# A fused linear-attention and gated-unit kernel: fixed engine orders, a gate on four array tiles, row loads for two batches, and zero products during the fill

## The chip, the cores and the metric

One core of one Trainium2 chip. The metric is the device time of one execution in microseconds (us), the median of several executions. Engines: PE multiplies matrices (PEld is its weight load, which overlaps with products: 203.6 us of PE and 143.5 of PEld in the span of 248.5 before), DVE is VectorE, ACT is ScalarE, POOL is GpSimd, SP only issues transfers. A run counts as slow when it is more than 1.5% above the fastest run of the same kernel on that chip. Executions scatter by some 2% here (four of the kernel before took 247.9 to 254.9 us), so this label often marks ordinary scatter.

## The reference

```python
def phi(x):                                    # x: [8 batches, 8 heads, 576, 64]
    proj = np.einsum('bhsd,df->bhsf', x, w_phi)                    # w_phi: [64, 128]
    proj = proj - np.max(np.abs(proj), axis=-1, keepdims=True)
    return np.concatenate([np.exp(proj), np.exp(-proj)], axis=-1)
q_p, k_p = phi(q), phi(k)
kv = np.einsum('bhsf,bhsd->bhfd', k_p, v)                          # the "state"
num = np.einsum('bhsf,bhfd->bhsd', q_p, kv)                        # the "numerator"
x = num / (den + 1e-6)                                             # -> [8, 576, 512]
for k in range(5):                                                 # causal convolution in time
    gate_pre += conv_w[k] * xp[:, k:k + S, :]
return (sigmoid(gate_pre) * (x @ w_val)) @ w_out                   # float32 [8, 576, 512]
```

## The kernel before

Python code lists some 1200 operations with their dependencies; a planner gives each an engine and a place in that engine's order, then they are emitted with semaphores. An engine's instructions are emitted in the order of its list, and one that waits holds up those behind it. Per batch: k and q come transposed into SBUF, are projected and exponentiated (KTIL, QTIL on ACT), v is scaled (VT, on POOL), PE forms the state (KV) and numerator (NUM), transposes it (XT), then come gate (GATE), value (VAL) and output (OUT). "Fill" below is the time until the first numerator product.

Batch 0 gets k and q as plain rows, with PE transposes; a copy from PSUM then writes every ninth element (1.95 us for 384 of them on DVE). All other batches are cast to bfloat16 into DRAM by a POOL transfer and read back by a transposing transfer.

```python
def load(b):
    if b == 0:
        ...   # row load XF, cast XB, PE transpose T0, copy T0c with stride 9
    else:
        pl.op("cast", "POOL", ...)     # k, q -> bf16 in DRAM
        pl.op("tr", "SP", ...)         # DRAM -> KT / QT, transposed
...
def mlp(b):
    for jt in range(4):
        def mm(E, at, jt=jt):          # gate: 12 products of 288 columns, two column tiles
            return [E.matmul(m.PS[ROWS[hh], at + p, 0:HALF], m.DG[:, 2 * jt + hh, 3 * p + dl, :],
                XT[:, 2 * jt + hh, dl:dl + HALF], start=(dl == 0), stop=(dl == 2), ...)
                for p in range(2) for dl in range(3) for hh in range(2)]
```

## Time and profile before

| | before |
|---|---|
| median of 4 executions | 250.2 us (247.9 to 254.9) |
| span of the profiled execution | 248.5 us |
| first numerator product | 55.7 us |
| end of PE | 241.3 us |

How to read it: the kernel is a pipeline over batches. Time until the first numerator is the fill, in which PE waits; from then to its end PE is nearly always busy, so each microsecond it saves there counts; then come 7 us of last copies and stores. The prediction shows the lines that carry this.

### The profile page before, as it was taken

How to read it: one execution, taken by the hardware profiler on the slowest of the kernel's cores; microseconds unless marked ns; L12 is line 12 of the kernel's file. 1: busy time of each engine (PE TensorE's matmuls, PEld its weight loads, DVE VectorE, ACT ScalarE, POOL GpSimd, SP SyncE). 2: the span in 40 equal slices, each digit the busy share in tenths (PEclk: the TensorE clock that was granted, in tenths of full speed). 3: DMA queues.
4: the chain of work that ended last, by engine and by line, in shares of the span. 5: the costliest groups of instructions: out<-in, count | busy, mean ns of one | idle time of the engine just before them, and what ended most of it. 6: DMA issues, size and time to landing. Idle time of an engine off the chain costs nothing.

```text
span 248.5 us, 8457 instructions
## 1 busy us (share of the span) xinstructions
PE 203.6 (82%) x3708; PEld 143.5 (58%) x3708; DVE 183.3 (74%) x276; ACT 184.9 (74%) x250; POOL 120.5 (48%) x206
## 2 busy tenths in 40 slices
PE   2124357599879999999999999999949999999970
PEld 1022234377675668657765876686626866776720
DVE  2399599539469967996998799789954799368460
ACT  5356989989915789898989899989497988982300
POOL 7274049639820883668138818652386064700000
PEclk9999999999999999999999999999997999999996
DMA  6992492998699959795899599978996524003132
GB/s 242 275 176 92 79 278 40 156 182 131 102 193 218 264 106 287 183 223 135 196 184 256 112 286 143 165 200 212 206 211 119 171 73 146 0 10 122 45 108 103
DMA packets 54398, 39.94 MB, mean 161 GB/s; under 512 B 39381, under 2 KB 48725, under 8 KB 53850
## 3 DMA queue, kind: packets, MB, share of 16 engines
q1 hardware_dynamic: 52240, 30.03, 50.3%
q0 software_dynamic: 1952, 9.31, 21.8%
q8 instruction: 29, 0.48, 0.8%
q10 hardware_dynamic: 170, 0.08, 0.1%
q14 instruction: 7, 0.06, 0.1%
HBM read 30.48 MB, written 17.69 MB: 194 GB/s over the span
## 4 chain that ended last, share of the span: by engine, by line
PE 50%; ACT 15%; DVE 13%; DMA 11%; SPq 4%; POOL 2%; issue 2%; ACTq 0%; DVEq 0%
PE PS L909 10%; PE PS L936 8%; DMA VN<-in_v_dram 7%; PE PS L898 7%; PE PS L785 5%; ACT KTIL L617 5%; ACT QTIL L744 5%; PE PS L822 4%; DVE MQb L704 4%; DMA wtmp<-in_w_phi_dram 3%; DVE QT L587 3%; DVE MK L612 3%; PE PS L731 3%; PE PS L691 2%; ACT GS L904 2%; PE PS L607 2%
## 5 line engine op out<-in xcount | busy, mean ns | idle before, releaser
L653 POOL TENSOR_TENSOR VT<-VN,EK 128x512 bf16<-128x512 f32 x64 | 65.7, 1045 | 18.6 <-DMA VN<-in_v_dram 15.1
L617 ACT ACTIVATE KTIL<-PS 128x1024 bf16<-128x1024 f32 x64 | 62.9, 1039 | 11.3 <-PE PS L607 8.3
L744 ACT ACTIVATE QTIL<-PS 128x1024 bf16<-128x1024 f32 x64 | 62.5, 1028 | 4.5 <-PE PS L737 3.7
L704 DVE TENSOR_REDUCE MQb<-PS 128x8 bf16<-128x1024 f32 (+1 forms) x40 | 44.2, 1110 | 11.9 <-PE PS L691 8.7
L612 DVE TENSOR_REDUCE MK<-PS 128x8 f32<-128x1024 f32 x32 | 38.7, 1216 | 8.6 <-ACT KTIL L617 4.5
L914 DVE SCALAR_TENSOR_TENSOR GV<-GS,PS 128x576 bf16<-128x576 bf16 x32 | 24.0, 751 | 17.7 <-PE PS L909 12.8
L909 PE MATMUL PS<-XT,WV 64*128 64x288 bf16 x512 | 35.7, 284 | 1.1 <-ACT OS L585 0.4
L641 POOL TENSOR_SCALAR MK<-MK 128x16 f32<-128x16 f32 (+1 forms) x24 | 6.0, 251 | 59.8 <-DVE MK L612 48.6
L936 PE MATMUL PS<-WO,GV 128*128 128x512 bf16 x128 | 32.1, 380 | 0.2 <-DVE XT L845 0.2
L898 PE MATMUL PS<-XT,DG 128*64 128x288 bf16 x384 | 28.6, 297 | 0.8 <-ACT GS L904 0.5
L909 PEld LDWEIGHTS PS<-XT,WV 64*128 64x128 bf16 x512 | 24.3, 94 | 7.8 <-issue 0.9
L904 ACT ACTIVATE GS<-PS 128x576 bf16<-128x576 f32 x32 | 20.8, 664 | 8.4 <-PE PS L898 6.0
L898 PEld LDWEIGHTS PS<-XT,DG 128*64 128x64 bf16 x384 | 20.5, 112 | 8.6 <-DVE XT L879 1.3
L691 PE MATMUL PS<-W,QT 64*128 64x128 bf16 x256 | 14.6, 239 | 10.7 <-ACT QT L585 4.0
L836 DVE TENSOR_TENSOR XN<-PS,RC 128x512 bf16<-128x512 f32 x32 | 21.9, 689 | 0.7
L607 PE MATMUL PS<-W,KT 64*128 64x128 bf16 x256 | 13.9, 240 | 10.0 <-DVE KT L587 7.0
L785 PE MATMUL PS<-VT,KTIL 128*128 128x65 bf16 x512 | 20.7, 196 | 0.2
L785 PEld LDWEIGHTS PS<-VT,KTIL 128*128 128x128 bf16 x512 | 18.9, 99 | 1.5 <-issue 0.5
L822 PEld LDWEIGHTS PS<-KVSB,QTIL 128*128 128x128 bf16 x512 | 17.3, 97 | 3.8 <-ACT QTIL L744 0.7
L822 PE MATMUL PS<-KVSB,QTIL 128*128 128x65 bf16 x512 | 19.3, 193 | 0.0
L585 ACT ACTIVATE OS<-PS 128x512 f32<-128x512 f32 x23 | 13.9, 609 | 6.2 <-PE PS L936 6.2
L691 PEld LDWEIGHTS PS<-W,QT 64*128 64x128 bf16 x256 | 8.8, 103 | 15.5 <-issue 8.3
(77 smaller groups left out, 298.2 us busy)
## 6 DMA issues: line engine op xcount, KB each, us to landing
VN<-in_v_dram SPq DMA_DIRECT2D x16, 512.0 KB, 7.4
out_dram<-OS SPq DMA_DIRECT2D x32, 256.0 KB, 3.1
R<-in_q_dram POOLq DMA_DIRECT2D x14, 288.0 KB, 6.3
R<-in_k_dram POOLq DMA_DIRECT2D x14, 288.0 KB, 5.6
QTIL<-in_k_dram SPq DMA_DIRECT2D x2, 576.0 KB, 5.7
QTIL<-in_q_dram SPq DMA_DIRECT2D x2, 576.0 KB, 8.4
VNt<-in_v_dram SPq DMA_DIRECT2D x32, 32.0 KB, 3.4
out_dram<-OS SPq DMA_DIRECT2D x16, 64.0 KB, 2.7
```

Source lines behind the costliest of these rows:

```text
L612: pl.op("Kmax", "DVE", dve(1024), lambda E, at, u=u: [E.tensor_reduce(MK[:, 0, 8 * u:8 * u + 8].rearrange("p (t x) -> p t x", t=2), m.PS[: ...
L617: pl.op("Kexp", "ACT", act(1024), lambda E, at, u=u, g=g: [E.activation(KTIL[:, g, u, :, :, :], m.PS[:, at:at + 2, :].rearrange("p t (x f) ...
L653: pl.op("VT", "POOL", pool(512), lambda E, at, u=u, hh=hh, a=a, g=g, EK=EK: [E.tensor_tensor(m.VT[s][:, g, u, :, :, 0:D], m.VN[s][:, 4 * h ...
L691: res.append(E.matmul(m.PS[:, at + par, P * x:P * x + P], QT[ROWS[par], 4 * hh + x, P * j:P * j + P], m.W2[ROWS[par], :], start=True, stop ...
L704: pl.op("Qmax", "DVE", dve(256 * nx), lambda E, at, u=u, nx=nx: [E.tensor_reduce(MQb[:, :].rearrange("p (t s) -> p t s", t=2)[:, :, 4 * u: ...
L744: pl.op("Qexp", "ACT", act(1024), lambda E, at, u=u, g=g: [E.activation(m.QTIL[s][:, g, u, :, :, :], m.PS[:, at:at + 2, :].rearrange("p t ...
L785: res.append(E.matmul(m.PS[:, at + sg, x * E1:(x + 1) * E1], m.KTIL[s][:, sg, 2 * g + a, par, x, :], m.VT[s][:, sg, 2 * g + a, par, x, :], ...
L822: return [E.matmul(m.PS[:, at + g, x * E1:(x + 1) * E1], m.QTIL[s][:, sg, 2 * j + g, par, x, :], m.KVSB[s][:, g, sg, x, :], start=(sg == 0 ...
L898: return [E.matmul(m.PS[ROWS[hh], at + p, 0:HALF], m.DG[:, 2 * jt + hh, 3 * p + dl, :], XT[:, 2 * jt + hh, dl:dl + HALF], start=(dl == 0), ...
L904: pl.op("TANH", "ACT", act(576), lambda E, at, GS=GS: [E.activation(GS[:, :, :], m.PS[:, at:at + 2, 0:HALF], AF.Tanh, scale=0.5)], pr, w=[ ...
L909: return [E.matmul(m.PS[:, at + p, 0:HALF], m.WV[ROWS[p], h, P * jt:P * jt + P], XT[ROWS[p], h, PAD:PAD + HALF], start=(h == 0), stop=(h = ...
L936: return [E.matmul(m.PS[:, at, :], m.GV[jt][:, s, p, P * j:P * j + P], m.WO[:, jt, :], start=(jt == 0), stop=(jt == 3)) for jt in range(4)]
```

## The change

Four intents: (1) the orders of all engines come from a search and are written into the kernel, with earliest times for transfers; (2) the gate uses 64x64 tiles, meant to run four at once, so that each of the five taps is multiplied once instead of six padded ones (20 products for 12 a tile, in two phases that add into the same PSUM banks); (3) batches 0 and 1 come by row loads and PE transposes whose copies are contiguous; (4) PE multiplies zeros while it waits in the fill, meant to keep its pace up: in the fill of the kernel before, eight products of L737 take 0.43 us, at 58.7 us 0.24. Some copies also move from DVE to ACT. Cut to its core:

```diff
-    pl.weigh(CFG)
-    pl.schedule(CFG["limit"], CFG["bonus"])
+    pl.schedule(ORDER, LATE)              # five lists of operation numbers, earliest times of transfers
...
-        if b == 0:
+        if b < 2:                         # row loads, PE transposes, contiguous copies
...
+            for n in range(4):            # two tiles y, each in phase 1 (taps 0, 2, 4) and phase 2 (1, 3)
+                y, ks = n % 2, ((0, 2, 4), (1, 3))[n // 2]
+                def mm(E, at, jt=2 * a + y, ks=ks):
+                    for k in ks:
+                        for hh in range(2):
+                            for par in range(2):
+                                h, dl = 2 * jt + hh, k // 2 + (k & 1) * (1 - par)
+                                res.append(E.matmul(m.PS[ROWS[hh], at + (par ^ (k & 1)), 0:HALF],
+                                    m.DG[ROWS[par], h, k, :], XT[ROWS[par], h, dl:dl + HALF],
+                                    start=(k == 0), stop=(k == 3), ...))
+                ... mode="T", sync=gate[-2:-1] if n > 1 else []   # phase 2 waits for its phase 1
...
+    def warm(E, k):                       # 137 of these, all before 40 us of the plan
+        E.matmul(m.PS[:, 7, 0:2 * P], m.Z[0:k, 0:P], m.Z[0:k, :], start=True, stop=True, ...)
```

## The prediction

> **What bounds the kernel now.** I read the page first (busy shares and the 40 slices), then sums over stretches of the span, then the chain that ended last in order of time, then the groups of instructions by form. From the page:
>
> ```profile
> PE 203.6 (82%) x3708; PEld 143.5 (58%) x3708; DVE 183.3 (74%) x276; ACT 184.9 (74%) x250; POOL 120.5 (48%) x206
> ...
> PE   2124357599879999999999999999949999999970
> ...
> ACT  5356989989915789898989899989497988982300
> ...
> DMA  6992492998699959795899599978996524003132
> ```
>
> No engine is near 100% over the span, but the PE row splits it: a fill of some nine slices of 6.2 us in which PE is mostly idle, then nines with one dip (slice 30), then the end. The sums over stretches (columns: stretch, its length, then busy us and instructions of PE, PEld, DVE, ACT, POOL; granted clock; DMA share; GB/s) give the sizes:
>
> ```profile
> 43.00:56.00 13.00, 9.96 (x181) 7.30 (x177) 6.24 (x8) 11.74 (x15) 7.14 (x13) 1.00 1.01 167
> 56.00:81.00 25.00, 22.30 (x443) 16.59 (x436) 19.21 (x32) 16.28 (x25) 13.56 (x24) 1.00 0.95 163
> 131.00:156.00 25.00, 24.47 (x480) 17.02 (x477) 21.80 (x35) 23.34 (x34) 16.59 (x29) 1.00 0.92 195
> 181.00:200.00 19.00, 15.62 (x292) 11.32 (x293) 11.98 (x15) 16.52 (x23) 9.41 (x17) 0.91 0.69 150
> ```
>
> In the steady stage PE is busy 24.5 of 25 us, so the PE stream is the bound there. Asked for 81 to 181 us as one stretch, PE is busy 98.55 of 100 us with 1908 products; the eight batches have about 455 each (3708 less the setup, divided by 8), so a batch takes 23.8 us. DVE and ACT are at 86% there and DMA at 93%: three followers are close behind. In the fill the chain of waits is another one (start, us, what):
>
> ```profile
> 2.05 8.48 DMA wtmp<-in_w_phi_dram
> ...
> 10.90 3.44 DVE KT L587 x2
> ...
> 16.27 3.43 DVE QT L587 x2
> ...
> 20.48 1.88 ACT QT L585
> ...
> 23.48 3.54 ACT KT L585 x2
> ...
> 43.23 0.43 PE PS L737 x8
> ...
> 54.91 0.71 DVE KVSB L799
> ...
> 58.71 0.24 PE PS L737 x8
> ```
>
> The reader sees: the projection weight lands only at 10.5 us; then transposed copies of k and q go one after another; the first numerator product (L856) starts at 55.66 us. The same eight products of L737 take 0.43 us in the fill and 0.24 us at 58.7. The groups carry the unit costs:
>
> ```profile
> L587 DVE COPY QT<-PS 128x384 bf16<-128x384 bf16 x4 | 7.0, 1949 | 0.0
> L845 DVE COPY XT<-PS 128x1024 bf16<-128x1024 bf16 x16 | 10.8, 682 | 0.4
> L898 PE MATMUL PS<-XT,DG 128*64 128x288 bf16 x384 | 28.6, 297 | 0.8 <-ACT GS L904 0.5 <-DVE XT L845 0.3
> L476 ACT ACTIVATE EB<-I 128x2304 bf16<-128x2304 bf16 x1 | 2.1, 2122 | 0.0
> ```
>
> [...] sixteen products of L822 take 0.59 us after another mode and 0.49 us after their own, so 0.1 us. No run yet shows four tiles at once. [...] The copies of L587 write every ninth element and take 1949 ns for 384 elements, against 682 ns for 1024 contiguous ones at L845. That is 7.6 times as much an element, [...] I use the measurement.
>
> **The change part by part.**
>
> *Row loads and PE transposes for batches 0 and 1.* Removed: 12 strided copies at 1.9 us, 13.5 us of it on DVE (7) and 9 on ACT (5); four of 28 casts to DRAM and four of 28 DMA transposes (batch 1). Added: 24 copies of contiguous halves, 16 of 512 elements and 8 of 128. Batch 0's twelve casts stay but go mostly to POOL (7 of 12, where 3 were). From L845, 512 elements cost DVE about 0.35 us, or 0.6 for the q halves, whose order changes; ACT about 0.5. In all some 9 us for both engines instead of 22.6. The broadcast table of 2304 columns (2.1 us on ACT) becomes a broadcast view. The weight is loaded first, on a queue ahead of q. So the first exponential, 15.5 us before, should come at about 7.5: load landed 4.5 (as the first k load does now, at 4.4), cast, transpose, copy and product with 0.5 to 1 us each.
>
> From there ACT sets the fill. In the new order it has, ahead of the first numerator, the 16 exponentials of k of batches 0 and 1 and 2 tails each (about 17 us at 0.93 dense and 0.5), those of q of batch 0 (8.4), some of q of batch 1 (3), about 11 copies (5) and small ones (1.5): 35 us. 7.5 + 35 + 1.5 for waits gives 44 us for the first numerator, in place of 55.7. That is **11.7 us**, nearly all of it on the path. ACT has no room to do better, so the zero products (137) and the warm clock by themselves are worth little, 1 us: PE waits for ACT in the fill, warm or not.
>
> *The gate.* Per tile of 128 channels, 12 products of 288 columns on two column tiles (0.86 us with the switch, 0.75 without) become 20 on four tiles. Five taps by 288 columns at the rate of the value product (16 products of 288 in 0.99 us, two at a time, so 123 ns per pair) make 0.62 us, 31 ns a product; the trace issues one each 30 ns in L785, so issue just holds. 32 x 0.12 = **3.8 us**, all on the PE stream, the bound of the steady stage. I expect PE busy in this group to fall from 28.6 to about 23 to 25 us.
>
> *Order.* Mode changes on PE are 174 before and 168 after, and after the first numerator 153 and 141: 12 x 0.11 = **1.3 us**. The work behind the first numerator, each product at its dense rate and each change at 0.11, comes to 172.8 us before and 167.4 after. Before, it took 185.7 us (55.7 to 241.4): 7.5% over. About 5 us of that are one stall, 181 to 192, where the v load lands at 178 and PE waits, then runs cold. New orders start loads at chosen points and should lose most of that stall. At 3 to 4% over, 167.4 becomes about 173 us.
>
> *Moved.* Seven of 16 state copies, five of eight small ones and four output copies go from DVE to ACT: some 7 us less on DVE, 5 more on ACT. Neither is the steady bound.
>
> *Sum.* 44 + 173 + 7.1 (end of PE to end of span, as before) = 224 us of span. Measured times lie about 2 us over the span (250.5 for 248.5), but the order tables were searched and may overlap more than I count. I say **225 us**.
>
> **The rivals.**
> *DMA becomes the bound.* It is 93% busy in the steady stage, some 22.2 us of DMA a batch; PE work falls to about 22.5 to 23. If loads queue, v lands late and the stall at 181 returns, perhaps twice, at 5 us each: 230 to 235. For it: two waits of 9 us on v in the chain. Against: batch 1's DRAM round trip is gone, and loads are timed.
> *The fill starves.* Each engine's order is fixed, batches 0 and 1 are interleaved, and three queues load at once. If batch 1's row loads are late, transposes of batch 1 hold up products of batch 0 on PE. The first numerator then comes at 48 to 52 us: 229 to 233. Against: 4.7 MB of inputs at some 250 GB/s are in by 20 us, and PE needs batch 1 only after all of batch 0's k.
> *The tiles don't overlap.* If only two of the four tiles run at once, 20 products take 1.2 us a tile in place of 0.75, and 32 tiles lose 15 us instead of gaining 4: 240 or so. For it: no trace of this kernel has four tiles. Against: two column tiles do overlap now.
> *ACT becomes the bound.* Its dense work is about 180 us (128 exponentials at 0.93, 32 tails at 0.5, 32 gates at 0.55, 27 output copies at 0.5, some 14 of small ones); with 7.5 before and 20 behind it is 208 at least, so it can't set the end unless it waits a lot. This is also the floor of any gain.
>
> **Range and chances.** The fill is fairly sure (8 to 14 us), the gate (0 to 4) and the stall (0 to 6) less so, and the order could give some us beyond. All good makes 215; fill and stall bad makes 236. The three runs of before spread from 247.9 to 254.9, so a miss of 2 us is noise. A time within 2% or above needs the gate to fail badly and the fill to starve. Faster 0.97, same 0.02, slower 0.01.
>
> **What would show it.** Right: first numerator at 42 to 46 us; copies into KT and QT at 0.3 to 0.65 us in place of 1.9; the gate at some 0.6 us per 20 products; no stretch after 60 us with PE below 90%; steady batch at 22.5 to 23.3 us; L737's successors as short in the fill as later. Wrong: DMA at 1.0 over many slices with PE waiting on VT or KT; PE waiting in the fill for batch 1's loads; gate products over 45 ns each; a low granted clock in the middle.

44 us to the first numerator, 173 to the end of PE and 7.1 behind it make 224 us of span, and the time said was 225. 0.11 us for a mode change, an estimate, agrees with the gate's 0.86 less 0.75 us; the products of L822 gave 0.1.

## More of the kernel before

One more stretch of the fill before, from the sums over stretches (columns: stretch, length, busy us and instructions of PE, PEld, DVE, ACT, POOL, granted clock, DMA share, GB/s), matters later:

```profile
6.00:43.00 37.00, 15.40 (x208) 10.13 (x210) 29.27 (x30) 27.05 (x33) 17.01 (x29) 1.00 0.65 158
```

While it fills, the DMA share of the kernel before is 0.65.

## The result, and the profile after

The changed kernel takes 236.9 us in the median (236.6 to 239.0, four fast runs) against 250.2 us. The ratio is 0.9515, 95% interval 0.942 to 0.961; a ratio here is the mean time of one kernel's fast runs over that of the other's fast runs of the same rounds, so not quite the ratio of the medians. So it is faster by 5%, and 12 us slower than forecast. The profiled execution (236.6 us) splits like this:

| part of the span, us | before | forecast | after |
|---|---|---|---|
| start to first numerator | 55.7 | 44 | 50.3 |
| first numerator to end of PE | 185.6 | 173 | 177.0 |
| end of PE to end of span | 7.2 | 7.1 | 7.5 |
| span | 248.5 | 224 | 234.8 |
| time over span | 2 | 1 | 1.8 |

Rows of the 40 slices of the kernel after:

```profile
PE   7679996698998999999999999999999999999970
...
ACT  0689989389999999999995999999967887833230
...
PEclk9999999589999999999999999999999999999995
DMA  5999999989991999999999999991513001411261
```

PE's dip at slice 30 is gone and PE is dense behind slice 9. But DMA is at 8 or 9 from slice 1 to 26, but for slice 12, and PE's clock has a dip in slices 7 and 8. The sums over stretches, columns as above:

```profile
6.00:43.00 37.00, 29.16 (x443) 19.70 (x441) 28.26 (x49) 32.47 (x46) 27.91 (x47) 0.99 1.24 206
43.00:56.00 13.00, 11.69 (x224) 9.40 (x225) 5.96 (x12) 8.44 (x12) 12.62 (x22) 0.77 1.06 173
56.00:81.00 25.00, 22.41 (x494) 15.53 (x494) 23.09 (x33) 24.27 (x36) 13.04 (x23) 1.00 0.95 192
131.00:156.00 25.00, 24.26 (x478) 16.56 (x478) 21.63 (x32) 24.28 (x37) 15.93 (x26) 1.00 1.08 241
181.00:200.00 19.00, 18.90 (x393) 13.26 (x391) 12.78 (x23) 15.42 (x20) 2.98 (x5) 1.00 0.05 17
```

The DMA share of the fill rose from 0.65 to 1.24 (it sums overlapping packets, so it can pass 1): the new order starts weights, batch 1's rows, and seven casts of batches 2 and 3 in there. In 6 to 43 us these casts land a median 11.7 to 11.9 us after issue, where the median over the whole run is 7.0 to 7.3. And the stretch 181 to 200 us, in which PE had 15.6 of 19 us before, is full. The chain of waits in the fill (start, us, what):

```profile
22.16 10.95 DMA VN<-in_v_dram
33.11 0.07 issue
33.18 1.04 POOL VT L638
...
37.62 1.94 POOL VTt L648 x2
...
40.56 0.68 POOL DG L463
...
41.69 0.39 PE PS L773 x7
42.08 1.45 issue
43.52 0.68 PE PS L773 x9
```

Not ACT but v sets the first state product in this run: its second load takes 11 us and lands at 33 us, POOL scales v piece by piece until 41.6 (with 0.7 us for one of the gate's diagonals, DG, in between), PE starts the state, and stops after seven products for 1.45 us with no semaphore to wait for. Then PE is at half pace, "cold" below (16 products of L773 take 1.09 us as busy time, and 0.90 from the first to the next product's start; 0.66 and 0.49 in a run below that stays warm), and the granted clock is 0.50 from 43 to 48 us. ACT, which the forecast named as the pace of the fill, had finished the work counted for it at 42.5 us and then waited 3.5 us for PE. Unit costs after, by form:

```profile
L897 PE MATMUL PS<-XT,DG 64*64 64x288 bf16 x640 | 26.4, 289 | 0.9
L569 DVE COPY KT<-PS 128x512 bf16<-128x512 bf16 x5 | 2.0, 412 | 2.2 <-PE PS L517 2.2
L567 ACT ACTIVATE QT<-PS 128x512 bf16<-128x512 bf16 x5 | 2.9, 599 | 0.5 <-PE PS L517 0.5
```

The copies are nearly as cheap as forecast (0.41 and 0.60 us for 1.95, where 0.35 and 0.5 were said; the q halves on DVE 0.68, where 0.6 was said; 10.6 us in all for both engines against 9). The gate is at 26.4 us of busy time, not at 23 to 25.

### The profile page after: what moved, and what is told of

Its sections match the earlier page's. It is cut to its first block, busy times and chain, and to the rows that moved or that the text cites. A ratio compares the mean times of both kernels' runs of the same rounds, so it can differ in the third digit from the quotient of the medians.

```text
span 234.8 us, 9303 instructions
## 1 busy us (share of the span) xinstructions
PE 211.1 (90%) x4112; PEld 147.7 (63%) x4129; DVE 171.7 (73%) x270; ACT 184.2 (78%) x268; POOL 125.6 (53%) x209
## 4 chain that ended last, share of the span: by engine, by line
PE 70%; DMA 9%; DVE 6%; ACT 5%; POOL 4%; issue 3%; ACTq 1%; DVEq 0%; SPq 0%
PE PS L917 14%; PE PS L897 11%; PE PS L946 10%; PE PS L773 7%; PE PS L811 6%; DMA VN<-in_v_dram 5%; DMA QTIL<-in_q_dram 5%; PE PS L676 3%; PE PS L830 3%; PE PS L719 3%; DVE MK L596 2%; PE PS L725 2%; ACT QTIL L732 2%; PE PS L590 2%; POOL VT L638 2%
## 5 line engine op out<-in xcount | busy, mean ns | idle before, releaser
L596 DVE TENSOR_REDUCE MK<-PS 128x8 f32<-128x1024 f32 x32 | 38.8, 1216 | 2.9 <-PE PS L590 1.5
L946 PE MATMUL PS<-WO,GV 128*128 128x512 bf16 x111 | 28.4, 379 | 2.7 <-issue 1.4
L917 PEld LDWEIGHTS PS<-XT,WV 64*128 64x128 bf16 x512 | 23.3, 94 | 8.1 <-DVE MQb L689 0.9
L567 ACT ACTIVATE OS<-PS 128x512 f32<-128x512 f32 x27 | 16.2, 606 | 15.5 <-PE PS L946 12.1
L897 PE MATMUL PS<-XT,DG 64*64 64x288 bf16 x640 | 26.4, 289 | 0.9
L773 PE MATMUL PS<-VT,KTIL 128*128 128x65 bf16 x512 | 21.6, 198 | 3.3 <-POOL VTt L652 1.7
L773 PEld LDWEIGHTS PS<-VT,KTIL 128*128 128x128 bf16 x512 | 19.4, 100 | 5.3 <-issue 2.5
L1058 PE MATMUL PS<-Z 128*128 128x256 bf16 (+1 forms) x137 | 20.8, 293 | 1.3 <-DVE Z L443 1.3
L897 PEld LDWEIGHTS PS<-XT,DG 64*64 64x64 bf16 x640 | 15.0, 105 | 9.4 <-PE PS L897 3.7
L946 PEld LDWEIGHTS PS<-WO,GV 128*128 128x128 bf16 x128 | 10.6, 97 | 11.6 <-issue 1.6
L648 POOL TENSOR_TENSOR VTt<-VNt,EK 128x512 bf16<-128x512 f32 x16 | 16.4, 1039 | 0.1
L1058 PEld LDWEIGHTS PS<-Z 128*128 128x128 bf16 (+1 forms) x137 | 13.0, 104 | 4.6 <-DVE Z L443 1.3
```

What stands on the lines that cost most here:

```text
L596: pl.op("Kmax", "DVE", dve(1024), lambda E, at, u=u: [E.tensor_reduce(MK[:, 0, 8 * u:8 * u + 8].rearrange("p (t x) -> p t x", t=2), m.PS[: ...
L773: res.append(E.matmul(m.PS[:, at + sg, x * E1:(x + 1) * E1], m.KTIL[s][:, sg, 2 * g + a, par, x, :], m.VT[s][:, sg, 2 * g + a, par, x, :], ...
L897: res.append(E.matmul(m.PS[ROWS[hh], at + (par ^ (k & 1)), 0:HALF], m.DG[ROWS[par], h, k, :], XT[ROWS[par], h, dl:dl + HALF], start=(k == ...
L917: return [E.matmul(m.PS[:, at + p, 0:HALF], m.WV[ROWS[p], h, P * jt:P * jt + P], XT[ROWS[p], h, PAD:PAD + HALF], start=(h == 0), stop=(h = ...
L946: return [E.matmul(m.PS[:, at, :], m.GV[jt][:, s, p, P * j:P * j + P], m.WO[:, jt, :], start=(jt == 0), stop=(jt == 3)) for jt in range(4)]
L1058: E.matmul(m.PS[:, 7, 0:2 * P], m.Z[0:k, 0:P], m.Z[0:k, :], start=True, stop=True, skip_group_check=True)
```

## The experiments

Each edit is against the changed kernel unless said otherwise. Operation numbers in order lists are given names. All ran correctly unless said otherwise.

### First call: the gate and the second v load

**Yardstick: the changed kernel, unaltered.**

> The changed kernel unaltered, as the common yardstick of these four runs. Every theory expects 236 to 239 us, span about 235, first numerator product (sixteen products of 65 columns into the numerator) at about 50.3 us, and the gate at about 28 us of PE time in all.

236.3 us (234.6 to 237.8). First numerator 48.6 us, with a hole of 1.06 us at the same product.

**The gate undone.** The old 12 products on two column tiles, in two pieces where the new pieces stood:

```diff
-                        m.PS[ROWS[hh], at + (par ^ (k & 1)), 0:HALF], m.DG[ROWS[par], h, k, :], ...
+                        m.PS[ROWS[hh], at + p, 0:HALF], m.DG[:, 2 * jt + hh, 3 * p + dl, :], ...
-                        mode="T", sync=gate[-2:-1] if n > 1 else []
+                        mode="C"                     # and DG, CWT with six taps again
```

> The gate alone undone: again 128-row products on two column tiles, 12 per tile of 128 channels, no wait between phases; the order tables stay. Theory A (the four-tile gate gives back its gain in the waits between its two phases): the gate takes about the same PE time as in the changed kernel (28 us in all), so the total stays within 1.5 us of it. Rival B (the step of the prediction: four tiles save 0.12 us a tile, 3.8 us in all, on the engine that is the bound): the total is 3 to 4 us longer, 240 to 241 us.

239.4 us (235.5 to 241.8; its profile counts as slow). The time from the start of one PE group to the start of the next, summed over the gate, is 26.7 us where the yardstick has 25.7 and the kernel before 27.7. So the new gate is worth about 1 us of PE against this one, and 2.0 us against the kernel before, where about 1.2 us of the gate's time came from products that ran cold in the stall at 187 us (24 products in 2.96 us, granted clock 0.50 in 186 to 188 us; 12 take 0.86 elsewhere). The rest of the 3 us between the medians is not gate: 2.2 of it are holes like the one at 42 us (below). The totals show nothing here: three of the four runs are slow, and the one fast run took 235.5 us, within the yardstick's range.

**Gate pieces sorted.** In eight of sixteen pairs of tiles the order puts a second phase right behind its own first. Here the pieces of each pair stand as first, first, second, second:

```diff
-  PE: ... 207 209 208 210 ...     # tile A phase 1, A phase 2, B phase 1, B phase 2
+  PE: ... 207 208 209 210 ...     # A1 B1 A2 B2; the same for all pairs
```

> Only the order of the gate's four pieces is changed where the second phase of a tile follows directly on its first (8 of 16 pairs): now first phase of both tiles, then second phase of both. Theory A: these 8 pairs take 14.5 us of PE in the changed kernel where well ordered pairs take 1.4 us each, so PE gets up to 3.5 us back, and the total falls by 1 to 3.5 us. Rival C (the search put them so because the second tile's PSUM banks come free late): pairs still take 1.7 us or more, now with PE waiting for ACT or DVE, and the total is the same or longer.

237.7 us (237.5 to 238.6). So the forecast gain of 1 to 3.5 us did not come. The gate fell to 24.0 us, but PE's idle time behind the first numerator (all waits over 0.15 us) rose from 4.2 to 6.4. The badly and the well ordered pair in the timeline of the changed kernel (start, us, ...; 40 products are two tiles):

```profile
60.26 1.95 PE L897 MATMUL PS<-XT,DG 64*64 64x288 bf16 x40
...
165.35 1.45 PE L897 MATMUL PS<-XT,DG 64*64 64x288 bf16 x40
```

What this wait costs in all, from PE's waits ("for what: us, times, longest"):

```profile
PEld PS L897 <- PE PS L897: 3.7, 10, 0.4
```

So the four tiles do overlap, 0.7 us a tile against 0.75 to 0.86 before, and half of the pairs lose that again to the wait between phases. Taking the wait away moves it elsewhere.

**The second v load of batch 0 at once.**

```diff
-LATE = {... 75: 18.95, ...}      # v.0.0 not before 18.95 us of the plan
+LATE = {...}
```

> The second v load of batch 0 is no longer held back until a transpose of batch 1 is done (it was issued at 22.1 us and landed at 33.1, and POOL waited 3.5 us for it); it is issued right behind the first one at about 10.5 us. Theory D (this late load, through POOL's multiplications and then KV, sets the fill): first numerator at 46 to 48 us, total 2 to 3.5 us shorter. Rival E (the DMA engines are saturated from 6 to 31 us, so what comes earlier pushes another load back): first numerator within 1 us of 50.3, total the same, with q or batch 1 loads landing later.

237.4 us (236.1 to 239.7). The second load landed at 23.8 us, 9.3 us earlier than in the first profile, and PE no longer waited for v, which was ready at 39.3 (41.2 in the yardstick). Yet the first state product came only at 40.4, 1.3 us earlier than in the first profile, and the hole in PE grew to 2.9 us: first numerator 50.7. The chain of waits now runs over DVE's maxima of q and PE's own list (L1058 are its zero products):

```profile
32.77 5.23 DVE MQb L689 x5
...
39.45 0.87 PE PS L1058 x7
40.38 0.37 PE PS L773 x7
40.74 2.90 issue
43.64 0.68 PE PS L773 x9
```

So v's late load alone is worth 1.3 us at most; another chain ends right behind it. There is also a first sign that the hole ends at a fixed time, not after a fixed wait.

### What the hole is

The profile's list of DMA queues (packets, MB, share), first after, then before:

```profile
q8 instruction: 32, 0.52, 0.9%
```

```profile
q8 instruction: 29, 0.48, 0.8%
```

Every one of these packets is 16384 bytes in both traces. PE has 4112 + 4129 = 8241 and 3708 + 3708 = 7416 products and weight loads, which is 258 and 256 for each packet. So this queue very likely carries PE's program while the kernel runs, some 256 instructions a packet (an estimate from these counts). If a hole is a late packet, holes must lie some 256 instructions or a multiple of it apart, whatever the kernel. I counted products ahead of each hole with no semaphore, leaving out waits of 0.16 to 0.18 us ahead of output products: 470, 597, 721 to 727, 851, 976 or 977, 1102, 1228 to 1230, 1356, 1481 to 1484, 1733 to 1738, 1992, 2114 to 2121, 2241 to 2247, 2367 to 2374, 2501 and 2622 to 2630, in the 19 traces of the kernel before, the changed one, and all variants (the lower ends are from traces that lack some records of output products). That is a grid of about 127 products (254 instructions, and a few that are no products). Even the one hole of the kernel before lies on it, at 727:

```profile
73.83 0.28 PE L691 MATMUL PS<-W,QT 64*128 64x128 bf16 x3 [1.34 <-issue]
```

The traces also hold the time of every packet of this queue. In the 19 traces all 65 holes over 0.19 us end 1.2 to 1.8 us (1.4 in the mean) after a packet of this queue has landed, though these packets come some 6 us apart (6.2 in the mean behind the fill of the first profile). So a hole is an instruction packet that landed late. Some of them (us):

| run | hole at product | packet, start to landing | PE goes on | hole |
|---|---|---|---|---|
| before | 727 | 71.41 to 72.37 | 73.83 | 1.34 |
| changed, first profile | 470 | 40.32 to 42.02 | 43.52 | 1.45 |
| second v load at once | 470 | 40.91 to 42.17 | 43.64 | 2.90 |
| twelve zeros more (below) | 470 | 35.07 to 40.97 | 42.35 | 1.62 |
| three casts later, at 33 us (below) | none | 35.70 to 36.80 | 41.20 | 0 |

With less traffic in the fill this packet comes earlier: it landed at 40.9 to 42.2 us in the nine profiles of the changed kernel and of variants with its casts, and at 36.8 to 39.0 in all seven in which three casts go out later, none of which has a hole there. Two runs of the new kernels stand apart: "four scalings of v on VectorE" (36.3 us, though the casts are in their old places) and "no zeros", whose stream is shorter.

### Second call: lighter fill, no zeros, v on VectorE

This call had no unaltered changed kernel on its chip, so its medians serve only for coarse comparison (before there: 252.0).

**No zero products.** `for _ in range(o.warm)` became `range(0)`.

> The changed kernel without its 137 zero products. Theory (the fill ends late because the data engines are saturated from 6 to 43 us, so that v arrives late and also the next 256 instructions of PE, whose late arrival is the 1.06 to 2.9 us gap in which PE waits for no semaphore): all such gaps so far lie about 508 products (4 x 127) or a multiple of it apart, so the gap after product 470 moves with the stream, to about product 470 of the shorter stream, 137 products further on in the real work. The first 16 products of the state then run without a hole, the gap is in another place, shorter or not there at all; the products of the fill are cold (0.4 against 0.24 us for eight). Both work against each other: first numerator 48 to 50.5 us, total within 1% of the changed kernel, 235 to 239. Rival (the zero products are what gains in the fill, PE clock matters): the first numerator falls back by 3 us or more, 53 us, and the total to 240. Rival (the gap is a wait on data that the profile doesn't name): it stays after seven products of the state, whatever number of zero products ran.

240.6 us (238.9 to 244.0), over the expected 235 to 239. The decisive part is the place of the hole: there is none in the state of batch 0 now, and the holes are at 721, 1102, 1228, ... of the shorter stream, which are other operations. A wait for data would have stayed with its data. The first numerator came at 50.7 us, 0.4 to 3.1 us later than in the four runs of the changed kernel (47.6 to 50.3).

**Three casts of batch 3 behind batch 0's v.**

```diff
-  POOL: ... 239 383 27 ... 20 385 ... 241 379 151 ... 258 128 284 ...
+  POOL: ... 239 27 ... 20 ... 241 151 ... 258 128 383 385 379 284 ...   # 383 385 379: casts of batch 3
-  SP:   ... 242 380 384 247 386 248 382 526 ...
+  SP:   ... 242 247 248 380 384 386 382 526 ...          # their transposes behind v of batch 2
```

> Three of the casts of batch 3 to DRAM (about 1.3 MB of traffic of some 8.6 MB in the fill) are issued after batch 0's v is scaled, about 42 us, instead of at 15 to 26 us; the transposes of batch 3 stand behind the v loads of batch 2. Theory (data engines saturated in the fill): everything behind them lands earlier, the second v load at 29 to 31 us instead of 33, the instruction gap shrinks to under 1 us, the first numerator comes at 46 to 48.5 us (50.3 and 48.6 in two runs of the changed kernel), total 233 to 236 unless batch 3 now starves later. Rival (GpSimd's scaling of v and ScalarE set the fill): first numerator 48.5 to 50.5, total as the changed kernel, 236 to 238.

241.3 us (239.5 to 243.4; profile slow, by 1.6% over its fastest; its fast runs, 239.5 to 241.7, miss the expected 233 to 236 just as much). The fill did what the theory said: the first state product came at 40.5 us, no hole, warm, first numerator at 45.0. PE's timeline there:

```profile
40.47 0.66 PE L773 MATMUL PS<-VT,KTIL 128*128 128x65 bf16 x16 [0.22 <-POOL VTt L652]
...
41.08 0.65 PE L773 MATMUL PS<-VT,KTIL 128*128 128x65 bf16 x16
```

All of it and more was given back at 64 us, where batch 3 was not there. From the waits:

```profile
PE PS L590 <- DMA KT<-R: 7.2, 1, 7.2
```

The casts went out at 42 us, took up to 14 us, a transpose another 15. So this traffic can't simply be put off: at 15 to 26 us it crowds the fill, at 42 us it comes too late for batch 3.

**Four scalings of v on VectorE.** Both tail scalings (1.2 us each there) and two others moved from POOL's list to DVE's at 31 to 38 us.

> Four of the ten large scalings of batch 0's v (1.0 us each) go from GpSimd to VectorE, which waits at 36 to 45 us; the planner then places 169 instead of 137 zero products, so that the gap of PE should lie some 32 products earlier than the state's first. Theory (v lands late and GpSimd scales it one after another, 33.2 to 41.6 us): GpSimd is done at 37.5 to 39 us, the first state product comes 2.5 to 4 us earlier if PE's gap doesn't take it back, first numerator 46 to 48, total 233 to 235. Rival (PE's own stream after that and the instruction gap): first numerator 48.5 to 50.5, total 236 to 238.

239.4 us (237.8 to 241.3). A miss of the test: DVE was not free. Its tail scalings waited for ACT until 33.8 us, which held up the maxima of q behind them and so PE and ACT; the first state product came at 44.6 us, later than before.

**All three together.**

> The second v load of batch 0 directly behind the first, three casts of batch 3 later, four scalings of v on VectorE: all three together. Theory (saturated data engines and late v): first numerator 43 to 46 us, close to the 44 predicted with ScalarE as the bound of the fill, total 230 to 233, less than the changed kernel by 2% or more. Rival (something else on PE holds the fill): first numerator over 48, total 235 to 238.

240.7 us (239.7 to 244.1), first numerator 49.1. The same mistake on DVE hides what the casts give.

### Third call: the mended fill

**Yardstick.**

> The changed kernel as it is, as the yardstick for the three that follow on the same chip. Both theories: 236 to 238 us, first numerator 48.5 to 50.5 us, a gap of 1 to 1.5 us after product 470 (seven products into the first state), with no semaphore behind it.

234.9 us (231.1 to 241.1; profile slow, 1.7% over its fastest). First numerator 47.6, with a hole of only 0.35 us.

**Twelve more zero products straight ahead of the first state product.**

```diff
+            o.warm += 12 if o.seq == 184 else 0        # 184: first state group of batch 0
```

> Twelve more zero products straight ahead of the first state product (19 instead of 7), nothing else. PE waits there for v anyway, 40.0 to 41.7 us. Theory (the 256 instructions after product 470 arrive at 42.4 to 43.6 us[...]; the gap sits at a fixed place of the stream): the gap now falls among the zero products, the 16 state products run without a hole, and PE stays warm; but the instructions arrive at about the same time, so the state starts at 42.5 to 43 and gains only the warm clock: first numerator 47 to 49, total 0.5 to 1.5 us under the changed kernel. Rival (a data wait inside the state): a hole of over 1 us stays after seven state products.

236.8 us (234.3 to 237.5). The hole is among the zeros now, and the state runs whole and warm:

```profile
39.02 1.70 PE L1059 MATMUL PS<-Z 128*128 128x256 bf16 x14
42.35 0.71 PE L1059 MATMUL PS<-Z 128*128 128x256 bf16 x5 [1.62 <-issue]
42.89 0.65 PE L774 MATMUL PS<-VT,KTIL 128*128 128x65 bf16 x16
```

The stream stops after product 470 again, and goes on at 42.35 us, about when the others did (42.4 to 43.6). So the rival, a data wait inside the state, is out. The total did not fall by the expected 0.5 to 1.5 us (yardstick 234.9).

**The casts of batch 3 at 33 us.** As the three-cast run, but 8 us earlier, with SP's list untouched. One thing more differs from the changed kernel: the planner now puts 19 zero products ahead of the first state product, as in the run before.

```diff
-  POOL: ... 149 123 133 150 ...
+  POOL: ... 149 123 383 385 379 133 150 ...      # and taken out of their old places
```

> The three casts of batch 3 go out right after the first scaling that needs the second v load (about 33 us), 8 us before those of the run that delayed them to 42 us and starved at 65 us for 7 us. Everything else is as in the changed kernel, but for the planner's zero products (19 ahead of the first state product). Theory (the data engines bound the fill; casts are needed only some 30 us later): the first numerator at 45 to 47.5 us, the transposes of batch 3 land by 64 us so that PE loses under 2 us there, total 232 to 234.5. Rival (the casts' traffic is only shifted and comes back as a wait): PE waits 4 us or more for the transposed k of batch 3 at about 64 us, total 236 to 239.

234.5 us (233.1 to 236.2; 0.940 of before, 0.932 to 0.949). First numerator 45.9, no wait for batch 3. The fair comparison for the casts is the run with twelve more zeros (47.5), so they bring 1.6 us of it, one profile each.

**The same, with the second v load at once and two scalings on DVE at 38 to 42 us**, where it does wait:

> As the run before, and the second v load of batch 0 goes out behind the first, and two of its scalings run on VectorE in its idle time at 38 to 42 us. Theory (late v, then GpSimd, set the state): first numerator 43 to 46 us, total 231 to 233.5. Rival (ScalarE, done with batch 1's exponentials at about 42 us, and the load that comes back): no more than the run before.

234.3 us (233.1 to 239.8; 0.937, 0.932 to 0.943). First numerator 45.4: the fill is within 1.4 us of the forecast. The total is not below the yardstick's by more than the scatter.

### Fourth call: does it reach the end?

**Yardstick, five rounds.**

> The changed kernel as it is, five rounds, as the yardstick. 235 to 237.5 us, first numerator 47.5 to 50.5 us.

235.6 us (233.4 to 237.5; ratio 0.939, 0.930 to 0.949). First numerator 47.8.

**The last kernel again.**

> The kernel with three casts of batch 3 later (33 us), the second v load at once and two scalings on VectorE, once more with five rounds. Theory (the fill's gain is real and stays): first numerator 45 to 46 us, total 2 to 4 us, about 1.2%, under the changed kernel of the same rounds. Rival (the gain of the fill is given back behind it, because the order of the steady stage waits for its casts and loads): first numerator as said, total within 1 us of the changed kernel.

236.3 us (233.8 to 239.6; 0.942, 0.932 to 0.951). Not faster than the changed kernel of the same rounds. Its profiled run is slow (first numerator 47.9, behind it 182.5), so I rest nothing on it alone. But the same fill has now given 45.4 and 47.9, and 46.9 in the fifth call: a single profile's first numerator scatters by 2 us or so.

**The same with sorted gate pieces.**

> The same, with the four pieces of every pair of gate tiles in the order first phase, first phase, second phase, second phase, so that no second phase follows its own first. Theory (those waits are part of the 4 us that the stage behind the first numerator is over the forecast): PE's time in the gate falls from 25.7 to about 24.1 us, the total by 1 to 1.6 us. Rival (as in the first try with the unaltered fill: the wait is replaced by others, since the following operations are ready no sooner): gate as said, idle time up by as much, total within 0.7 us.

236.8 us (234.5 to 238.2; 0.944, 0.934 to 0.954). First numerator 45.7, gate 25.1 us, yet PE's time behind the first numerator is 182.0. I put the profiles beside each other, but for the kernel before, the stalled three-cast run, the slow one above and the two of the fifth call (us; "behind" is first numerator to end of PE, "holes" those of the grid behind the first numerator):

| kernel | profile | first numerator | behind | holes |
|---|---|---|---|---|
| changed, four runs | 3 fast, 1 slow | 50.3, 48.6, 47.6 (slow), 47.8 | 177.0, 177.9, 178.1, 177.7 | 0.6, 0.6, 1.2, 1.1 |
| gate undone | slow | 49.6 | 180.3 | 2.8 |
| gate sorted | fast | 48.3 | 180.1 | 1.4 |
| second v load at once | fast | 50.7 | 178.1 | 0.7 |
| twelve zeros more | fast | 47.5 | 179.8 | 3.1 |
| no zeros | fast | 50.7 | 181.3 | 4.8 |
| four scalings on DVE | fast | 48.9 | 179.6 | 1.8 |
| all three | fast | 49.1 | 181.2 | 4.5 |
| casts at 33 us | fast | 45.9 | 177.9 | 1.2 |
| the same, v at once, two on DVE | fast | 45.4 | 178.9 | 2.1 |
| the same, gate sorted | fast | 45.7 | 182.0 | 3.5 |

Across fast profiles, PE's time behind the first numerator grows roughly as the holes do: 181.2 to 182.0 where they sum to 3.5 to 4.8, against 177.0 to 178.9 where they sum to 0.6 to 2.1. Two lie above that line (gate sorted, four scalings on DVE). So the holes are one place where a mended fill or gate gives its gain back, not shown to be the only one.

### Fifth call: are the holes made by the DMA load?

**The stores of the first seven batches cut to 2 of 128 rows**, wrong results, in the changed kernel:

```diff
-   ob[p, P * j:P * j + P, :], OS[:, :]
+   ob[p, P * j:P * j + (P if b == B - 1 else 2), :], OS[0:(P if b == B - 1 else 2), :]
```

> The changed kernel with wrong results on purpose: the 28 large stores of the first seven batches write 2 of 128 rows each, 4 KB in place of 256 KB, about 7.2 MB less of some 39 MB. The fill has no stores, so the first numerator stays at 47.5 to 50.5 us. Theory (the holes of PE behind it are instructions that wait for loaded data engines): the DMA share of the stretches from 81 to 156 us falls from 1.03 to 1.13 to under 0.95, the holes behind the first numerator sum to under 0.4 us (0.4 to 1.2 in four runs of the changed kernel), PE's time from the first numerator to its end falls from 177.7 to 175.5 to 177, total 233 to 235.5. Rival (fetching has its own pace): holes and time as before, total 235 to 237.

238.1 us (235.4 to 239.7), 31.6 MB moved instead of 38.8. First numerator 49.2, behind it 178.4, holes 1.2. The DMA share of 81 to 131 us fell only to 0.97 to 0.99 (0.83 in 131 to 156).

**The same cut in the kernel with the mended fill.**

> The same cut of the stores in the kernel with three casts later, the second v load at once and two scalings on VectorE, whose holes behind the first numerator summed to 2.1 and 4.05 us in two runs. Theory: the holes sum to under 0.7 us, first numerator 45 to 47.5, PE's time behind it 176 to 178, total 230 to 233: the fill's gain now reaches the end. Rival: holes of 2 to 4 us stay, PE's time behind the first numerator 179 to 182, total 233 to 236.

237.7 us (235.1 to 239.6), first numerator 46.9, behind it 178.9, holes 2.1. The theory missed in both: with 19% fewer bytes the holes stayed (1.2 and 2.1, where under 0.4 and 0.7 were expected), one of them 1.73 us at product 2120. The packet records narrow it down: behind the first numerator the packets ahead of a hole took 0.9 to 1.6 us themselves, with the stores cut 0.9 to 1.0. What is late is their start, 3.2 to 6.2 us after the product some 127 places earlier (3.5 to 5.3 with the stores cut), while PE needs about 6 us for 127 products (5.3 to 8.2 behind the fill of the first profile). Why they start late, by the reading traffic, which kept DMA near 1 around the holes, or by a pace of their own, these runs don't tell.

## Why the prediction was wrong

The direction (faster), the parts that gain and most unit costs were right; 225 us was 12 us too low. On the profiled run: 6.3 us in the fill, 4.0 behind it, 0.4 at the end, 1.8 between span and time, less 1 that the forecast had added to its 224.

1. **"7.5 + 35 + 1.5 for waits gives 44 us for the first numerator": the step that failed.** Its second term held, by luck of two errors: the first exponential came at 10.1 us, not 7.5, and ACT was done at 42.5. But the assumption in it, that ACT sets the fill, did not hold. PE waited 1.7 us for v, then for a late instruction packet, and went cold.

   Of the 6.3 us in the first profile, by comparison with other runs (an estimate): 1.3 are v (first state product at 41.7, and 40.4 with v loaded early), 4.0 the hole and the cold clock (8.6 us from there to the first numerator, and some 4.6 in the runs without either), 1.0 is left in every variant. In the four runs of the changed kernel v's part is 0.9 to 2.9 and that of hole and clock 0 to 4.0.

   The step beneath was the argument against the rival "The fill starves": "4.7 MB of inputs at some 250 GB/s are in by 20 us" (the first two slices of the kernel before moved 242 and 275 GB/s). I counted k and q of batches 0 and 1, without v, and left out what the new order starts beside them: 7.6 MB moved in 6 to 43 us at 206 GB/s, and the DMA share went from 0.65 to 1.24. That rival's own figure, 48 to 52 us, is about what the four runs show (47.6 to 50.3), by luck: it named batch 1's rows as what comes late, and it was batch 0's v and PE's instructions. Two of the forecast's own signs of being wrong came true, PE waiting on VT beside a DMA share near 1, and a low clock (at 43 to 56 us).

   Moving three casts to 33 us brought the first numerator to 45.9, 1.6 us under the run with the same zeros, one profile each. Over all profiles it is 47.5 to 50.7 (mean 48.8) in the nine with the casts in their old places, and 45.0 to 47.9 (mean 46.1) in the six with three casts later (without the one that holds up VectorE). So moving them, with what came along in some of these runs, is worth some 2.7 us.
2. **"the zero products (137) and the warm clock by themselves are worth little, 1 us": mis-sized, in both directions.** In the first profile PE waited 1.7 us for v and, seven products later, 1.45 in the hole, and was then cold for some 5 us (granted clock 0.50 from 43 to 48 us, 0.55 in the next). From the first state product to the first numerator it took 8.6 us, against 4.1 to 4.6 where it stayed warm and whole, and 6.1 without zeros, where it was whole. The zeros stop at 40 us of the plan and so miss the very place; twelve more bring 4.6. Without any zeros the first numerator came at 50.7. The clock row, which showed nothing of the slow products in the fill of the kernel before (0.43 us for eight, granted clock 1.00 in 42 to 44 us), did show this one: 0.77 in 43 to 56 us.
3. **The gate, "32 x 0.12 = 3.8 us": half of it.** 2.0 us came (27.7 to 25.7, start to start). Well ordered pairs take 0.7 us a tile where 0.62 was forecast (34.5 ns a product, not 31), and eight of sixteen pairs wait for their own first phase, to which the forecast gave no cost. Where the order lets them, the tiles do overlap: 20 products take 0.7 us, where two at a time would take 1.2 (the forecast's estimate, ten pairs at 123 ns). The rival "The tiles don't overlap" (240 us) is out.
4. **"At 3 to 4% over, 167.4 becomes about 173 us": 177 to 178.** The stall at 181 to 192 us went, as said: PE's idle time behind the first numerator (waits over 0.15 us) fell from 8.5 to between 4.0 and 5.3 us. The excess left is idle time of that size, the gate's 1.8, and about 3 us more of products and switches over my dense rates that no run isolates. The late instruction packets, unforeseen, are part of the idle time: 0.6 to 1.2 us in the changed kernel, up to 4.8 in variants.
5. **Copies, load order, PE's switch count**: the copies nearly as forecast (0.41 and 0.60 us). The old ones of 384 elements with stride 9 took 1.91 to 1.95 us on DVE and 1.86 to 1.96 on ACT, so what the stride cost is not DVE's alone; why it costs that was not shown. And the switches are in the order's part of point 4.
6. **The rival "DMA becomes the bound" (230 to 235 us)** was half right: DMA share is at 0.95 to 1.12 from 56 to 156 us, but v does not stall the steady stage.
7. **"Measured times lie about 2 us over the span ... but the order tables were searched and may overlap more than I count"**: trading a known 2 us against a hope was a choice, and a wrong one.

What stays open: why the kernels with a mended fill end at 234 to 237 us, as the changed kernel does. The holes account for part of what is given back. That they are late instruction packets is shown, and that the one of the fill comes earlier when three casts go out later; why packets start late behind the fill is not.

## What to carry to other kernels

Before calling one engine the pace of a fill, add up every byte that the new order starts in it, not only the bytes that the fill needs, and ask what lands last; then test it, for the load that landed last was worth 1.3 us here, with another chain right behind it. A prefetch moved out of the way must still be there in time: the same three casts cost 7 us of stall when they went out 8 us later. And when a well-fed engine stops with no semaphore to wait for, count its instructions between such stops, and look up when the packets of the instruction queue landed, before looking for a data dependency.
